# One head and two blocks at a time: another shape of the score matmuls in a fused attention and two-MLP kernel

## The chip, the cores and the metric

The kernel runs on one core of one Trainium2 chip. The metric is the device time of one execution in microseconds (us). Three runs of the kernel before gave 885.55, 885.6 and 886.19 us, median 885.6.

## The reference

The program is a chain of three parts. Attention has 4 batches, 8 heads, 576 positions and head dimension 64, with a mask by blocks of 64: a query sees every key of its own block and of the blocks before it. Its output, 2304 rows of 512, goes through a layer with three input matrices, the elementwise maximum of the three products and an output matrix, and then through a layer with g = h * cos(h).

```python
scores = scale * np.matmul(q, k.transpose(0, 1, 3, 2))
mask = block_i >= block_j                      # block = position // 64
scores = np.where(mask, scores, -1000000000.0)
scores = scores - np.max(scores, axis=-1, keepdims=True)
attn = np.exp(scores)
attn = attn / (np.sum(attn, axis=-1, keepdims=True) + 1e-09)
x = np.matmul(attn, v)                         # then reshaped to (2304, 512)
h = np.maximum(np.maximum(x @ w1, x @ w2), x @ w3)
x = h @ w_out                                  # 512 -> 768 -> 512
h = x @ w_in
out = (h * np.cos(h)) @ w_out2                 # 512 -> 2048 -> 512
```

All data is fp32. The two layers and most scores are computed with each fp32 operand split in a high and a low part of type fp32r: high times high, high times low and low times high, three matmuls that add up in one PSUM tile.

## The kernel before

**How attention is tiled.** An item is one batch, one pair of heads and one half of the queries; there are 32, numbered by batch, then half, then pair. In batch one (b = 0) the halves are blocks 0 to 4 and 5 to 8; in the other three batches they are blocks 0 to 3 and 4 to 8 (the table `HALF`, lines 549 to 562). This text calls them the early and the later queries.

For a block of 64 queries, `q` is laid out in 128 columns: 64 of the first head, with zeros in the rows of the second, and 64 of the second, with zeros in the rows of the first. One matmul of that 128x128 operand against the keys of both heads (head one in rows 0 to 63, head two in 64 to 127) gives the scores of both heads for one block, and runs only over the keys that the block sees, 64 (b + 1) columns. No mask is needed. `scores` (line 611) makes three matmuls for each block (`qh` with `kh`, `qh` with `kl`, `ql` with `kh`), or one in plain fp32 for the first ten items (`NATIVE`, tiles `qnat` and `knat`). The scores stand in the PSUM tiles SA (two banks) and SB (one bank), one buffer each. VectorE takes the maxima (`top`), ScalarE the exponentials (`prob`, one tile for each block, and `sums`), and the rows are then scaled.

`transposes` (line 655) turns `prob` by 128x128 TensorE transposes, four to a PSUM tile `tb`, copied into `pt`: 6 for an item with blocks 0 to 3 and 19 for one with blocks 4 to 8. `pv` (line 668) multiplies `pt` with v (`vr`) in plain fp32 into the PSUM tile X: the first head into rows 0 to 63, the second into rows 64 to 127, which the profile shows as matmuls of form 128*64 instead of 128*128. Such a group is called a visit to v here. From batch two on, the early queries of two pairs share one visit (`twin`, `pv(items[n - 2], it)`).

**What else runs.** The first layer's matmuls (tile `psm`, function `moe1_units`) are interleaved with attention, a chunk of tokens as soon as its attention is done. The second layer follows (`psm` and `po`). Weights come from memory and are split by VectorE and ScalarE (`convert`, tiles `raw`, `t`, `whi`, `wlo`). `load` (line 579) brings q, k and v of an item two items ahead; `q`, `k`, `kh`, `kl`, `qh` and `ql` have one buffer each. `prep` (line 599) makes the high and low parts.

**What sets the order.** All operations are recorded first, each with its engine or engines, a price and the operations it needs. A planner (class `Plan`) then schedules the list several times forward and backward (`PASSES`), keeps the shortest plan by its prices, and issues the instructions of each engine in that order, which is fixed from then on. A group marked `unit()` stays together. The price of a visit to v holds 350 ns beside its matmuls (`SWITCH`, line 686); that of a transpose is 109 ns. All instructions are issued from the helper in line 214, so that they are told apart in the profile by their tiles.

Of the kernel before, what the change touches and what calls it, by code (L numbers as in the profile page):

```python
# [8 lines left out]
F32 = mybir.dt.float32  # L9
# [10 lines left out]
P = 128  # L20
# [5 lines left out]
def f32(ap):  # L26
    return ap.bitcast(F32)
# [102 lines left out]
class Plan:  # L130
# [155 lines left out]


    ENGINES = ("PE", "DVE", "ACT", "POOL", "SP")
    PASSES = 8

    def after(self, d, o, stop):
        if d.engine == "PE" and o.engine == "PE":
# [13 lines left out]
    def forward(self, rank):  # L306
# [6 lines left out]
        end, chosen, bus, port = {}, {}, 0.0, 0.0  # L313

        def finish(o, start, stop):
            nonlocal left
            left -= 1
# [24 lines left out]
        left = len(self.ops)  # L342
        for o in self.ops:
            if not o.deps:
                release(o)
        while left:
            best = None
            for e in free:
                while waiting[e] and waiting[e][0][0] <= free[e]:
                    at, r, order, o = heapq.heappop(waiting[e])  # L350
                    heapq.heappush(ready[e], (r, order, at, o))
                if ready[e]:
                    t, pick = free[e], ready[e][0]
                    if pick[3].port and port > t:
                        others = [x for x in ready[e] if not x[3].port]
                        if others:
                            pick = min(others)
                        else:
                            t = port
                elif waiting[e]:  # L360
                    pick = waiting[e][0]
                    t = max(pick[0], port if pick[3].port else 0.0)
                else:
                    continue
                if best is None or t < best[0]:
                    best = (t, e, pick)
            assert best, "the plan has a cycle"
            t, e, pick = best
            o = pick[3]
            if ready[e]:  # L370
                ready[e].remove(pick)
                heapq.heapify(ready[e])
            else:
                heapq.heappop(waiting[e])
            free[e] = t + self.spent(o, t)
            load[e] -= o.cost
            stop = free[e] + o.late
            if o.port:
                port = free[e]
            if e == "SP":  # L380
                bus = max(bus, t + o.cost)
                bus += (o.late - 2000.0) * (1.22 if bus < self.SLOW else 1.0)
                stop = bus + 2000.0
            finish(o, t, stop)
# [73 lines left out]
                fn()  # L458


def fused_kernel(tc, qk, v2, w1, w2, w3, wout, w_in2, w_out2, out):
    B, HP, _, S = qk.shape
    S //= 3
    D = P // 2
# [79 lines left out]
    class Half:  # L544
        pass

    HALF = []
    for first, last, *tiles in (  # L550
# [5 lines left out]
        f = Half()  # L556
        f.first, f.blocks, f.tiles = first, list(range(first, last)), tiles
        f.n = 64 * (last - first)
        f.nk = 64 * last
        f.nj = (last + 1) // 2  # L560
        f.order = [(j, b) for j in range(f.nj) for b in f.blocks if 64 * (b + 1) > 128 * j]
        HALF.append(f)
    NATIVE = 10

    items = []
    for b in range(B):
        for half in range(2):
            for pair in range(HP):
                it = Item()
                it.b, it.half, it.pair, it.n, it.f = b, half, pair, len(items), HALF[half + 2 * (b > 0)]  # L570
# [4 lines left out]
    prob = [at.tile([P, (b // 2 + 1) * P], F32, f"prob{b}") for b in range(S // 64)]  # L575
    for b in range(0, S // 64, 2):
        R.gpsimd.memset(prob[b][:, 64 * (b + 1):], 0.0)

    def load(it):
# [8 lines left out]
        nlow = 2 * HALF[2 * (it.b > 0)].n  # L588
        q0 = nlow + S if it.half else 0
        R.sync.dma_start(it.q, src[:, q0:q0 + nq])  # L590
        R.sync.dma_start(it.k, src[:, nlow:nlow + f.nk])
        if it.n == 0:
            conv_next()
        it.j0 = f.nj if it.twin and it.pair % 2 else 0
        it.vr = items[it.n - 1].vr if it.j0 else at.tile([P, 5, 2, 64], F32, "vr", tag="vr", bufs=2)
        R.sync.dma_start(it.vr[:, it.j0:it.j0 + f.nj].rearrange("p j a d -> p j (a d)"),
                         v2[it.b, it.pair, :, 0:f.nj])

    def prep(it):
        f = it.f  # L600
        if it.native:
            R.scale(it.k, it.k, scale)
            return
# [4 lines left out]
        R.scale(it.qh, it.q, scale)  # L608
        R.vector.scalar_tensor_tensor(it.ql, it.q, scale, f32(it.qh), ALU.mult, ALU.subtract)

    def scores(it):

        f = it.f
        sm = sums[it.n % NROT]
        nb = len(f.blocks)
# [37 lines left out]
            R.scale_rows(p, p, sm[:, i:i + 1])  # L653

    def transposes(it):
        order = it.f.order
        it.c0 = len(order) if it.j0 else 0
        it.pt = items[it.n - 1].pt if it.j0 else at.tile([P, 19, P], F32, "pt", tag="pt")
        for c in range(0, len(order), 4):
            part = order[c:c + 4]  # L660
            n = P * len(part)
# [4 lines left out]
            R.copy(it.pt[:, it.c0 + c:it.c0 + c + len(part)].rearrange("p b n -> p (b n)"), t[:, :n])  # L666

    def pv(*its):
        f = its[0].f
# [4 lines left out]
        X = ps_x.tile([P, 512], F32, "X", tag="X")  # L674
        with R.unit():
            for x, it in enumerate(its):
                for j in range(f.nj):
                    c0, b0 = where[j][0]
                    q0 = 64 * (b0 - f.first)
                    for e in range(2):  # L680
                        a = 64 * e
                        p = it.pt[:, it.c0 + c0:it.c0 + c0 + len(where[j]), a:a + 64]
                        R.tensor.matmul(X[a:a + 64, x * n + q0:x * n + n], it.vr[:, it.j0 + j, e], p,
                                        start=x == 0 and j == 0, stop=x == len(its) - 1 and j == f.nj - 1,
                                        skip_group_check=True)
            R.unit_op.cost += R.SWITCH
        t0 = S * it.b + HALF[2 * (it.b > 0)].n * it.half
        for x, it in enumerate(its):
            xs = None
            for c, to, frm, m in pieces(t0, n):  # L690
                src = X[:, x * n + frm:x * n + frm + m]
                if c == 0:
                    h, l = xhi[0][it.pair][:, to:to + m], xlo[0][it.pair][:, to:to + m]
                    R.copy(h, src)
                    R.vector.tensor_tensor(l, src, f32(h), ALU.subtract)
                else:
                    xs = xs or at.tile([P, NLOW], F32, "xs", tag="xs", bufs=2)
                    R.copy(xs[:, frm:frm + m], src)
                    R.sync.dma_start(x_dram[c][it.pair][:, to:to + m], xs[:, frm:frm + m])

    def load_x(c, k):
        n = parts[c][1]
# [114 lines left out]
    for n in range(NI + 1):  # L817
        if n:
            transposes(items[n - 1])
        for step in range(3):  # L820
# [3 lines left out]
                    load(items[n + LA])  # L824
            if step == 2 and n:
                it = items[n - 1]
                if not it.twin:
                    pv(it)
                elif it.j0:
                    pv(items[n - 2], it)  # L830
                if it.n == HP - 1:
                    R.close(cv_start)
                    wk = R.open(cv_start, name="wk", bufs=1)
                done = S * it.b + (S if it.half else it.f.n) if it.pair == HP - 1 else 0
# [181 lines left out]
```

## Time and profile before

| | us |
|---|---|
| median of three runs | 885.6 |
| profiled execution, its own time | 885.22 |
| span of its trace, first to last instruction | 883.4 |
| TensorE (PE) busy | 868.1 |
| VectorE (DVE) busy | 540.9 |
| ScalarE (ACT) busy | 440.7 |
| GpSimd (POOL) busy | 1.2 |

The busy time of PE counts a matmul from its start to its modelled end, and ends overlap the next starts: a matmul of 512 columns is shown with some 390 ns, while the next starts 227 ns later. How long the engine is held by one instruction is therefore read from the start of one row of the timeline to the start of the next, not from the mean durations. In the timeline, equal neighbours are merged into one row with xN. A plain fp32 matmul is two instructions there, a transpose is one. After a group of transposes the next matmul is shown with an early start and a longer stay.

### The profile page before, as it was taken

To read this page: it belongs to the slowest core of one execution; us is meant where nothing else is said; L and a number is where in the kernel's file an instruction comes from. 1 tells how busy PE (TensorE), PEld (TensorE's weight loads), DVE (VectorE), ACT (ScalarE), POOL (GpSimd) and SP (SyncE) were. 2 spreads that over 40 slices of the span, in tenths; PEclk is the share of its full clock that TensorE was granted. 3 is DMA by queue.
4 is the path that set the end of the run, shared out by engine and by line. 5 is a ranking of instruction groups with operands and counts; after the bars stand their busy time and mean duration, and the time that the engine had idled before them with its cause. 6 is when DMAs were issued, how large, how long until landed. Compare 5 with 4: busy or idle time off the path is not lost.

```text
span 883.4 us, 12430 instructions
## 1 busy us (share of the span) xinstructions
PE 868.1 (98%) x4618; PEld 721.1 (82%) x4618; DVE 540.9 (61%) x1072; ACT 440.7 (50%) x969; POOL 1.2 (0%) x12
## 2 busy tenths in 40 slices
PE   7899999999999999999999999999999999999998
PEld 5568888888888888888899888888888888888897
DVE  6999986774566635628522897645564555555454
ACT  7997687853777627845321543332233223322333
POOL 0000000000000000000000000000000000000000
PEclk9999999999999999999999999999999999999999
DMA  7765545662256503355030931110001000100000
GB/s 259 233 203 174 151 151 175 217 228 77 75 155 220 207 1 106 129 171 167 23 122 17 354 130 48 48 48 1 0 24 49 1 0 1 48 1 0 25 24 24
DMA packets 42396, 90.33 MB, mean 102 GB/s; under 512 B 5728, under 2 KB 15456, under 8 KB 42336
## 3 DMA queue, kind: packets, MB, share of 16 engines
q1 hardware_dynamic: 42336, 89.54, 31.0%
q8 instruction: 36, 0.59, 0.3%
q14 instruction: 24, 0.20, 0.1%
HBM read 69.07 MB, written 20.45 MB: 101 GB/s over the span
## 4 chain that ended last, share of the span: by engine, by line
PE 93%; DVE 3%; ACT 2%; DMA 1%; issue 0%; POOLq 0%; POOL 0%; ACTq 0%
PE psm L214 56%; PE po L214 22%; PE X L214 4%; PE tb L214 4%; PE SA L214 4%; PE SB L214 3%; ACT prob L214 1%; DVE t L214 1%; DVE top L214 1%; DMA raw<-w 0%; ACT pt L214 0%; DVE prob L214 0%; DMA knat<-qk 0%; ACT t L214 0%; DVE whi L214 0%
## 5 line engine op out<-in xcount | busy, mean ns | idle before, releaser
L214 PE MATMUL psm<-yh,w_in 128*128 128x512 f32 (+1 forms) x640 | 194.2, 368 | 0.0
L214 PE MATMUL po<-w_out,gh 128*128 128x512 f32 x576 | 177.7, 390 | 0.0
L214 ACT ACTIVATE th<-th,halfpi 128x512 f32<-128x512 f32 (+1 forms) x80 | 54.5, 682 | 189.0 <-DVE th L214 189.0
L214 PE MATMUL psm<-xhi,whi 128*128 128x512 f32 (+1 forms) x360 | 135.4, 376 | 0.0
L214 PEld LDWEIGHTS psm<-yh,w_in 128*128 128x128 f32 x640 | 117.1, 188 | 20.8
L214 PE MATMUL psm<-xhi,wlo 128*128 128x512 f32 (+1 forms) x360 | 132.7, 369 | 0.0
L214 PE MATMUL psm<-xlo,whi 128*128 128x512 f32 (+1 forms) x360 | 132.6, 368 | 0.0
L214 PEld LDWEIGHTS po<-w_out,gh 128*128 128x128 f32 x576 | 107.1, 188 | 21.3
L214 PE MATMUL psm<-yl,w_in 128*128 128x512 f32 (+1 forms) x320 | 117.7, 368 | 0.0
L214 PE MATMUL po<-w_out,gl 128*128 128x512 f32 x288 | 112.0, 389 | 0.0
L214 DVE TENSOR_SCALAR th<-psm 128x512 int32<-128x512 f32 (+1 forms) x80 | 51.0, 637 | 76.4 <-PE psm L214 76.2
L214 DVE TENSOR_TENSOR th<-psm,th 128x512 f32<-128x512 f32 (+1 forms) x80 | 51.0, 637 | 53.7 <-ACT th L214 53.7
L214 DVE TENSOR_TENSOR hm<-psm,hm 128x512 f32<-128x512 f32 (+1 forms) x60 | 38.1, 634 | 66.7 <-PE psm L214 64.8
L214 PEld LDWEIGHTS psm<-xhi,wlo 128*128 128x128 f32 x360 | 67.9, 189 | 11.5
L214 PEld LDWEIGHTS psm<-xhi,whi 128*128 128x128 f32 x360 | 68.0, 189 | 10.3 <-issue 0.3
L214 PEld LDWEIGHTS psm<-xlo,whi 128*128 128x128 f32 x360 | 68.0, 189 | 9.8
L214 DVE TENSOR_TENSOR gl<-th,gh 128x512 fp32r<-128x512 f32 (+1 forms) x80 | 50.9, 636 | 38.3 <-ACT gh L214 38.3
L214 ACT CAST gh<-th 128x512 fp32r<-128x512 f32 (+1 forms) x76 | 44.0, 578 | 55.7 <-DVE th L214 55.7
L214 PEld LDWEIGHTS psm<-yl,w_in 128*128 128x128 f32 x320 | 60.3, 188 | 10.5
L214 ACT COPY pt<-tb 128x512 f32<-128x512 f32 (+1 forms) x96 | 52.9, 570 | 21.4 <-PE tb L214 20.9
L214 PEld LDWEIGHTS po<-w_out,gl 128*128 128x128 f32 x288 | 54.1, 188 | 11.4
L214 PE MATMUL tb<-ident,prob 128*128 128x128 f32 x400 | 57.6, 276 | 2.6 <-ACT pt L214 1.8
(96 smaller groups left out, 1305.0 us busy)
## 6 DMA issues: line engine op xcount, KB each, us to landing
raw<-w SPq DMA_DIRECT2D x18, 512.0 KB, 3.7
raw<-w_in SPq DMA_DIRECT2D x16, 512.0 KB, 4.0
raw<-w_out SPq DMA_DIRECT2D x16, 512.0 KB, 4.5
vr<-v SPq DMA_DIRECT2D x16, 320.0 KB, 3.4
kept_in<-both SPq DMA_DIRECT2D x10, 512.0 KB, 3.1
w_in<-kept_in SPq DMA_DIRECT2D x10, 512.0 KB, 9.9
out<-osb SPq DMA_DIRECT2D x18, 256.0 KB, 2.0
y<-hm SPq DMA_DIRECT2D x16, 256.0 KB, 2.8
```

The lines of the kernel that those rows point to most:

```text
L214: return lambda: getattr(real, method)(*[value(a) for a in args], **{k: value(a) for k, a in kw.items()})
```

## The change

From batch two on the halves are blocks 0 to 4 and 5 to 8, as in batch one, and the later queries (now four blocks) are computed in another way; their items are called stacked. q comes in 256 columns for each head (four blocks of 64), the same 64 rows twice. The scaled high part stands in `qh` rows 0 to 63 and the low part in rows 64 to 127; k of one head, twice too, is in `kh`. One matmul of `qh` with `kh` then gives high times high plus low times high. A second, `ql` with `kl`, has the high part of q and the low part of k in rows 0 to 63, and in rows 64 and 96 a mask: -2^100 in q's columns of the earlier block of two, 1 in the last 64 keys. A matmul takes two blocks of one head (128 columns of q) against all keys that the later block sees: blocks 5 and 6 against 448 keys in SB, blocks 7 and 8 against 576 keys in SA.

The two heads of an item follow each other: k of the second head has a load of its own and the same single-buffered tiles `k`, `kh` and `kl`. `kl` and `ql` stay in place over the four pairs of a batch, and their mask rows are set by GpSimd once for each batch. The transposes of a stacked item are 18, nine for each head: groups of four 128x128, and groups of five, of which two turn only the rows 64 to 127 of a tile, because the other rows are masked. Each item has its own visit to v. The planner makes 30 passes instead of 8.

```diff
-    PASSES = 8
+    PASSES = 30
...
+    PAIRS = ((0, P, 7 * 64, (6, 7)), (P, 2 * P, S, (8, 5)))
+    NEVER = -2.0 ** 100
...
-                it.twin = b > 0 and not half
                 it.native = it.n < NATIVE
+                it.stacked = b > 0 and half == 1
...
+            if it.stacked:
+                it.k = [it.k, at.tile([P, S], F32, "k", tag="k")]
...
+            for e in range(2):
+                R.sync.dma_start(it.k[e], k1[it.b - 1, it.pair, :, e * S:e * S + S])
...
+    def prep_k(it, e):
+        it.kh = at.tile([P, S], F32R, "kh", tag="kh")
+        R.copy(it.kh, it.k[e])
+        R.sub(it.kl[0:64], it.k[e][0:64], f32(it.kh[0:64]))
+
+    def prep_stacked(it):
...
+        it.qh = at.tile([P, 5 * P], F32R, "qh", tag="qh")[:, :4 * P]
+        R.scale(it.qh, it.q, scale)
+        R.copy(it.ql[0:64], f32(it.qh[0:64]))
+        R.vector.scalar_tensor_tensor(it.qh[64:P], it.q[64:P], scale, f32(it.qh[64:P]), ALU.mult, ALU.subtract)
+        prep_k(it, 0)
+
+    def scores_stacked(it):
+        sm = sums[it.n % NROT]
+        for e in range(2):
+            if e:
+                prep_k(it, 1)
...
+            for x, (q0, q1, nk, where) in enumerate(PAIRS):
...
+                for bank in range(c):
+                    with R.unit():
+                        for i, (q, k) in enumerate(((it.qh, it.kh), (it.ql, it.kl))):
+                            R.tensor.matmul(s[:, bank, 0:n], q[:, qs], k[:, bank * n:bank * n + n], start=i == 0,
+                                            stop=i == 1, skip_group_check=True)
...
+    def transposes_stacked(it):
+        it.pt = at.tile([P, 16 * P], F32, "pt", tag="pt")
+        for e in range(2):
+            a, b = (prob[where[e]] for *_, where in PAIRS)
+            for h in range(2):
+                tiles = [(a, 2 * h, 0), (b, 2 * h, 0)] + (
+                    [(a, 1, 0), (b, 1, 0)] if h == 0 else [(a, 3, 64), (b, 3, 0), (b, 4, 64)])
+                t = ps_x.tile([P, 512], F32, "tb", tag="T", bufs=2)
+                with R.unit():
+                    c0 = 0
+                    for p, j, r in tiles:
+                        R.tensor.transpose(t[:, c0:c0 + P - r], p[r:P, j * P:j * P + P], ident[r:P, r:P])
+                        c0 += P - r
+                c = 1024 * e + 512 * h
+                R.copy(it.pt[:, c:c + 512], t)
+
+    def pv_stacked(it):
+        X = ps_x.tile([P, 512], F32, "X", tag="X")
+        with R.unit():
+            for j, (c0, m) in enumerate(((0, 256), (256, 256), (512, 256), (768, 192), (960, 64))):
+                for e in range(2):
+                    p = it.pt[:, 1024 * e + c0:1024 * e + c0 + m]
+                    R.tensor.matmul(X[64 * e:64 * e + 64, 256 - m:256], it.vr[:, j, e], p, start=j == 0, stop=j == 4,
+                                    skip_group_check=True)
+            R.unit_op.cost += R.SWITCH
+        return X
...
-                if not it.twin:
-                    pv(it)
-                elif it.j0:
-                    pv(items[n - 2], it)
+                pv(it)
```

The three places below are all on TensorE. First the scores of an item of later queries in batch two. Before, SA holds blocks 8 (288 columns in each of two banks) and 6 (224), three matmuls each:

```order
L214 MATMUL SA<-kh,qh 128x288
L214 MATMUL SA<-kl,qh 128x288
L214 MATMUL SA<-kh,ql 128x288
L214 MATMUL SA<-kh,qh 128x224
L214 MATMUL SA<-kl,qh 128x224
L214 MATMUL SA<-kh,ql 128x224
L214 MATMUL SA<-kh,qh 128x288
L214 MATMUL SA<-kl,qh 128x288
L214 MATMUL SA<-kh,ql 128x288
L214 MATMUL SA<-kh,qh 128x224
L214 MATMUL SA<-kl,qh 128x224
L214 MATMUL SA<-kh,ql 128x224
```

Now the scores of the second head of a stacked item: two matmuls of 448 in SB, and twice two of 288 in SA.

```order
L214 MATMUL SB<-kh,qh 128x448
L214 MATMUL SB<-kl,ql 128x448
L214 MATMUL SA<-kh,qh 128x288
L214 MATMUL SA<-kl,ql 128x288
L214 MATMUL SA<-kh,qh 128x288
L214 MATMUL SA<-kl,ql 128x288
```

The three products of a block have become two of a pair of blocks, and what followed for blocks 7, 5 and 4 in further tiles is in these six as well.

Second, the transposes of such an item. Before, three groups of four and more stand between the scores, all of the whole 128 rows:

```order
L214 MATMUL tb<-ident,prob_430 128x128
L214 MATMUL tb<-ident,prob_102 128x128
L214 MATMUL tb<-ident,prob_98 128x128
L214 MATMUL tb<-ident,prob_463 128x128
```

Now the two groups of one head in batch two, with the matmuls of the first layer around them (a row of form 128x64 turns 64 rows):

```order
L214 MATMUL psm<-xhi_503,wlo_1_1128 128x512
L214 MATMUL tb<-ident,prob_100 128x128
L214 MATMUL tb<-ident,prob_102 128x128
L214 MATMUL tb<-ident,prob_100 128x128
L214 MATMUL tb<-ident,prob_102 128x128
L214 MATMUL tb<-ident,prob_100 128x128
L214 MATMUL tb<-ident,prob_102 128x128
L214 MATMUL tb<-ident,prob_100 128x64
L214 MATMUL tb<-ident,prob_102 128x128
L214 MATMUL tb<-ident,prob_102 128x64
L214 MATMUL psm<-xhi_255,whi_2_1144 128x512
```

The second group has five transposes instead of four, and the third and the fifth of it are of 64 rows.

Third, the visit to v of early queries in batch two, before with two items in it:

```order
L214 MATMUL psm<-xhi_2217,wlo_0_1069 128x512
L214 MATMUL X<-pt,vr 64x256 x2
L214 MATMUL X<-pt,vr 64x128 x2
L214 MATMUL X<-pt,vr 64x256 x2
L214 MATMUL X<-pt,vr 64x128 x2
L214 MATMUL tb<-ident,prob_98 128x128
```

And now with one item, of five blocks:

```order
L214 MATMUL SA<-kl,ql 128x288
L214 MATMUL X<-pt,vr 64x320 x2
L214 MATMUL X<-pt,vr 64x192 x2
L214 MATMUL X<-pt,vr 64x64 x2
L214 MATMUL psm<-xhi_503,whi_2_1144 128x512
```

The visit holds three pairs of matmuls in place of four, and there are two such visits for one before.

## Rows read from the trace of the kernel before

**Rows 1.** The page, part 1: busy us, share of the span, instructions by engine.

```profile
PE 868.1 (98%) x4618; PEld 721.1 (82%) x4618; DVE 540.9 (61%) x1072; ACT 440.7 (50%) x969; POOL 1.2 (0%) x12
```

**Rows 2.** Windows, core 0: each engine's busy us, granted TensorE clock, DMA.

```profile
0.00:75.00 75.00, 63.32 (x391) 46.79 (x392) 66.89 (x178) 67.23 (x181) 1.17 (x12) 1.00 0.71 226
75.00:395.00 320.00, 320.00 (x1867) 263.62 (x1866) 205.11 (x438) 212.83 (x517) 0.00 (x0) 1.00 0.47 150
395.00:875.00 480.00, 480.00 (x2344) 407.06 (x2343) 267.45 (x455) 158.51 (x268) 0.00 (x0) 1.00 0.15 52
875.00:883.00 8.00, 4.78 (x22) 3.60 (x20) 1.41 (x4) 2.09 (x4) 0.00 (x0) 0.98 0.18 66
```

**Rows 3.** Timeline, PE, one visit to v: start us, duration us, instruction.

```profile
239.23 0.39 PE L214 MATMUL psm<-xhi,whi 128*128 128x512 f32 x1
239.46 0.39 PE L214 MATMUL psm<-xlo,whi 128*128 128x512 f32 x1
239.68 0.39 PE L214 MATMUL psm<-xhi,wlo 128*128 128x512 f32 x1
240.00 2.27 PE L214 MATMUL X<-pt,vr 128*64 128x320 f32 x20
242.21 0.40 PE L214 MATMUL SA<-kh,qh 128*128 128x288 f32 x1
242.44 0.30 PE L214 MATMUL SA<-kl,qh 128*128 128x288 f32 x1
242.58 0.29 PE L214 MATMUL SA<-kh,ql 128*128 128x288 f32 x1
```

**Rows 4.** Timeline, PE, scores of a later-queries item and the transposes behind.

```profile
257.19 0.29 PE L214 MATMUL SA<-kh,qh 128*128 128x288 f32 x1
257.32 0.29 PE L214 MATMUL SA<-kl,qh 128*128 128x288 f32 x1
...
257.58 0.27 PE L214 MATMUL SA<-kh,qh 128*128 128x224 f32 x1
257.69 0.28 PE L214 MATMUL SA<-kl,qh 128*128 128x224 f32 x1
...
257.91 1.04 PE L214 MATMUL tb<-ident,prob 128*128 128x128 f32 x8
258.70 0.38 PE L214 MATMUL SA<-kh,qh 128*128 128x288 f32 x1
258.92 0.29 PE L214 MATMUL SA<-kl,qh 128*128 128x288 f32 x1
```

**Rows 5.** Timeline, PE, narrower scores of a later-queries item.

```profile
249.30 0.34 PE L214 MATMUL SB<-kh,qh 128*128 128x384 f32 x1
249.48 0.34 PE L214 MATMUL SB<-kl,qh 128*128 128x384 f32 x1
...
249.83 0.32 PE L214 MATMUL SB<-kh,qh 128*128 128x320 f32 x1
...
250.29 0.39 PE L214 MATMUL psm<-hh,vhi 128*128 128x512 f32 x1
```

**Rows 6.** Timeline, PE, plain fp32 scores of batch one.

```profile
16.18 1.08 PE L214 MATMUL SB<-knat,qnat 128*128 128x320 f32 x4
17.09 1.04 PE L214 MATMUL tb<-ident,prob 128*128 128x128 f32 x8
```

**Rows 7.** Groups by form: busy us, mean ns of one, idle before.

```profile
L214 DVE TENSOR_TENSOR kl<-k,kh 128x576 fp32r<-128x576 f32 x12 | 9.0, 754 | 1.1 <-ACT kh L214 1.1
L214 ACT CAST kh<-k 128x576 fp32r<-128x576 f32 x12 | 8.0, 670 | 4.5 <-PE SB L214 4.4 <-PE SA L214 0.2
L214 DVE SCALAR_TENSOR_TENSOR ql<-q,qh 128x512 fp32r<-128x512 f32 x10 | 6.8, 681 | 0.0
L214 POOL MEMSET prob<- 128x64 f32 x5 | 0.6, 153 | 0.0
```

**Rows 8.** Tile k: time from issue to landing of its 22 loads.

```profile
DMA to landing us min/median/max: 2.1/2.8/6.2
```

More of the change, by code (lines that the diff above doesn't have):

```diff
@@ L315, in finish @@
         def finish(o, start, stop):
-            nonlocal left
-            left -= 1
             end[o] = (start, stop)
@@ L340, in release @@
             heapq.heappush(waiting[o.engine], (at, rank[o], o.order, o))
-        left = len(self.ops)
         for o in self.ops:
@@ L345, in forward @@
                 release(o)
-        while left:
+        while len(end) < len(self.ops):
             best = None
@@ L549, in fused_kernel @@
     HALF = []
-    for first, last, *tiles in (
[5 rows of a table removed]
-        f = Half()
[L557 to L560, printed above, removed]
+    for u in range(2):
+        f = Half()
+        f.n = NHIGH if u else NLOW
+        f.first = 5 if u else 0
+        f.blocks = list(range(5, 9)) if u else list(range(0, 5))
+        f.nk = S if u else NLOW
+        f.nj = 5 if u else 3
+        f.both = 0 if u else 128
         f.order = [(j, b) for j in range(f.nj) for b in f.blocks if 64 * (b + 1) > 128 * j]
+        f.tiles = ((2, ((8, 0, 288, 2), (6, 288, 224, 2))), (1, ((7, 0, 512, 1),)), (1, ((5, 0, 384, 1),))) if u else (
+            (1, ((4, 0, 320, 1), (2, 320, 192, 1))), (0, ((3, 0, 256, 1), (1, 256, 128, 1), (0, 384, 64, 1))))
         HALF.append(f)
+    PAIRS = ((0, P, 7 * 64, (6, 7)), (P, 2 * P, S, (8, 5)))
+    NEVER = -2.0 ** 100
     NATIVE = 10
@@ L569, in fused_kernel @@
                 it = Item()
-                it.b, it.half, it.pair, it.n, it.f = b, half, pair, len(items), HALF[half + 2 * (b > 0)]
-                it.twin = b > 0 and not half
+                it.b, it.half, it.pair, it.n, it.f = b, half, pair, len(items), HALF[half]
                 it.native = it.n < NATIVE
+                it.stacked = b > 0 and half == 1
                 items.append(it)
-    prob = [at.tile([P, (b // 2 + 1) * P], F32, f"prob{b}") for b in range(S // 64)]
+    prob = [at.tile([P, (9 if b == 5 else b) // 2 * P + P], F32, f"prob{b}") for b in range(S // 64)]
     for b in range(0, S // 64, 2):
         R.gpsimd.memset(prob[b][:, 64 * (b + 1):], 0.0)
+    R.gpsimd.memset(prob[5][:, S:], 0.0)
     def load(it):
@@ L587, in load @@
             it.k = at.tile([P, S], F32, "k", tag="k")[:, :f.nk]
-        nlow = 2 * HALF[2 * (it.b > 0)].n
-        q0 = nlow + S if it.half else 0
+            if it.stacked:
+                it.k = [it.k, at.tile([P, S], F32, "k", tag="k")]
+        q0 = 2 * NLOW + S if it.half else 0
         R.sync.dma_start(it.q, src[:, q0:q0 + nq])
-        R.sync.dma_start(it.k, src[:, nlow:nlow + f.nk])
+        if it.stacked:
+            for e in range(2):
+                R.sync.dma_start(it.k[e], k1[it.b - 1, it.pair, :, e * S:e * S + S])
+        else:
+            R.sync.dma_start(it.k, src[:, 2 * NLOW:2 * NLOW + f.nk])
         if it.n == 0:
             conv_next()
[L594 to L597, printed above, removed]
+        it.vr = at.tile([P, 5, 2, 64], F32, "vr", tag="vr", bufs=2)
+        R.sync.dma_start(it.vr[:, 0:f.nj].rearrange("p j a d -> p j (a d)"), v2[it.b, it.pair, :, 0:f.nj])
     def prep(it):
         f = it.f
+        if it.stacked:
+            return prep_stacked(it)
         if it.native:
@@ L609, in prep @@
         R.vector.scalar_tensor_tensor(it.ql, it.q, scale, f32(it.qh), ALU.mult, ALU.subtract)
+    def prep_k(it, e):
[3 more added lines that the diff above has]
+    def prep_stacked(it):
+        if it.pair:
+            it.kl, it.ql = items[it.n - 1].kl, items[it.n - 1].ql
+        else:
+            it.kl = at.tile([P, S], F32R, "kl", tag="kl")
+            it.ql = at.tile([P, 5 * P], F32R, "ql", tag="ql")[:, :4 * P]
+            for t in (it.kl, it.ql):
+                R.gpsimd.memset(f32(t[64:P]), 0.0)
+            for x, (q0, q1, nk, _) in enumerate(PAIRS):
+                row = slice(64 + 32 * x, 65 + 32 * x)
+                R.gpsimd.memset(f32(it.kl[row, nk - 64:nk]), 1.0)
+                for e in range(2):
+                    R.gpsimd.memset(f32(it.ql[row, 2 * P * e + q0:2 * P * e + q0 + 64]), NEVER)
+            if it.b == 1:
+                R.gpsimd.memset(prob[7][:, 7 * 64:], 0.0)
+        it.qh = at.tile([P, 5 * P], F32R, "qh", tag="qh")[:, :4 * P]
[3 more added lines that the diff above has]
+        prep_k(it, 0)
@@ new lines, in transposes_stacked @@
+    def transposes_stacked(it):
+        it.pt = at.tile([P, 16 * P], F32, "pt", tag="pt")
+        for e in range(2):
+            a, b = (prob[where[e]] for *_, where in PAIRS)
[10 more added lines that the diff above has]
+                R.copy(it.pt[:, c:c + 512], t)
@@ new lines, in pv_stacked @@
+    def pv_stacked(it):
+        X = ps_x.tile([P, 512], F32, "X", tag="X")
+        with R.unit():
+            for j, (c0, m) in enumerate(((0, 256), (256, 256), (512, 256), (768, 192), (960, 64))):
+                for e in range(2):
+                    p = it.pt[:, 1024 * e + c0:1024 * e + c0 + m]
[3 more added lines that the diff above has]
+        return X
@@ L611, in scores @@
     def scores(it):
+        if it.stacked:
+            return scores_stacked(it)
         f = it.f
@@ L655, in transposes @@
     def transposes(it):
+        if it.stacked:
+            return transposes_stacked(it)
         order = it.f.order
-        it.c0 = len(order) if it.j0 else 0
-        it.pt = items[it.n - 1].pt if it.j0 else at.tile([P, 19, P], F32, "pt", tag="pt")
+        it.pt = at.tile([P, 16, P], F32, "pt", tag="pt")
         for c in range(0, len(order), 4):
@@ L665, in transposes, with pv @@
                     R.tensor.transpose(t[:, x * P:x * P + P], prob[b][:, j * P:j * P + P], ident)
-            R.copy(it.pt[:, it.c0 + c:it.c0 + c + len(part)].rearrange("p b n -> p (b n)"), t[:, :n])
-    def pv(*its):
-        f = its[0].f
+            R.copy(it.pt[:, c:c + len(part)].rearrange("p b n -> p (b n)"), t[:, :n])
+    def pv(it):
+        f = it.f
         n = f.n
@@ L673, in pv @@
             where.setdefault(j, []).append((c, b))
-        X = ps_x.tile([P, 512], F32, "X", tag="X")
-        with R.unit():
-            for x, it in enumerate(its):
+        if it.stacked:
+            X = pv_stacked(it)
+        else:
+            X = ps_x.tile([P, 512], F32, "X", tag="X")
+            with R.unit():
                 for j in range(f.nj):
@@ L681, in pv @@
                         a = 64 * e
-                        p = it.pt[:, it.c0 + c0:it.c0 + c0 + len(where[j]), a:a + 64]
-                        R.tensor.matmul(X[a:a + 64, x * n + q0:x * n + n], it.vr[:, it.j0 + j, e], p,
-                                        start=x == 0 and j == 0, stop=x == len(its) - 1 and j == f.nj - 1,
+                        p = it.pt[:, c0:c0 + len(where[j]), a:a + 64]
+                        R.tensor.matmul(X[a:a + 64, q0:n], it.vr[:, j, e], p, start=j == 0, stop=j == f.nj - 1,
                                         skip_group_check=True)
[L686 to L699, printed above, removed]
+                R.unit_op.cost += R.SWITCH
+        t0 = S * it.b + NLOW * it.half
+        xs = None
+        for c, to, frm, m in pieces(t0, n):
+            src = X[:, 0 + frm:0 + frm + m]
+            if c == 0:
+                h, l = xhi[0][it.pair][:, to:to + m], xlo[0][it.pair][:, to:to + m]
+                R.copy(h, src)
+                R.vector.tensor_tensor(l, src, f32(h), ALU.subtract)
+            else:
+                xs = xs or at.tile([P, NLOW], F32, "xs", tag="xs", bufs=2)
+                R.copy(xs[:, frm:frm + m], src)
+                R.sync.dma_start(x_dram[c][it.pair][:, to:to + m], xs[:, frm:frm + m])
     def load_x(c, k):
@@ L833, in fused_kernel @@
                     wk = R.open(cv_start, name="wk", bufs=1)
-                done = S * it.b + (S if it.half else it.f.n) if it.pair == HP - 1 else 0
+                done = S * it.b + (S if it.half else NLOW) if it.pair == HP - 1 else 0
                 while begun[0] < len(parts) and sum(parts[begun[0]]) <= done:
@@ L995 @@
     qd = qd.reshape(B, H // 2, P, 2 * S)
+    last = heads.reshape(B, H // 2, 2, D, S)[1:, ..., NLOW:].transpose(0, 1, 3, 2, 4).reshape(B - 1, H // 2, D, 2 * NHIGH)
+    qd[1:, :, :, 2 * NLOW:] = np.concatenate([last, last], axis=2)
+    k1 = kT[1:].reshape(B - 1, H // 2, 2, D, S).transpose(0, 1, 3, 2, 4).reshape(B - 1, H // 2, D, 2 * S)
     kT = kT.reshape(B, H // 2, P, S)
-    low = [2 * NLOW] + [2 * NHIGH] * (B - 1)
     arrays = {
-        "qk": np.stack([np.concatenate([qd[b, ..., :n], kT[b], qd[b, ..., n:]], axis=2) for b, n in enumerate(low)]),
+        "qk": np.concatenate([qd[..., :2 * NLOW], kT, qd[..., 2 * NLOW:]], axis=3),
+        "k1": np.concatenate([k1, k1], axis=2),
         "v2": np.ascontiguousarray(v2.reshape(B, H // 2, P, (S + D) // P, 2 * D)),
```

19 lines of the change are left out of this document (18 added, 1 removed), and 5 rows, old and new, of the table HALF.

## Prediction

> **What bounds the kernel now.** I read the page's engine shares first, then the busy time by stretches, then TensorE's timeline inside attention, and last the groups by form. The page shows PE busy in 98% of the span [rows 1]. By stretches the reader sees where the rest is [rows 2]: 11.7 us of the first 75 (75.00 less 63.32), nothing from 75 to 875 us, 3.2 us in the last eight. The granted clock is 1.00 from the start to 875 us, the upper level (2.4 GHz) throughout. The change begins with batch two, whose stacked items lie between about 100 us and the end of attention near 395 us. There PE is busy in 320.00 of 320 us, VectorE in 205 and ScalarE in 213. So PE sets the time in this stretch, and each us that an instruction holds PE, longer or shorter, moves the end by one us, as long as the others keep up. Busy time alone hides short gaps, so I count PE's time from start to start in the timeline.
>
> **Score matmuls.** The products of the first layer in front of a visit follow each other every 227 ns at 512 columns (239.23 to 239.68 for two) [rows 3]. Three of 288 columns take 0.39 us and three of 224 take 0.33 [rows 4]; three of 384 take 0.53 and three of 320 take 0.46 [rows 5]. An item of later queries before: block 7 (512) 0.68, block 5 (384) 0.53, block 4 (320) 0.46, block 8 (six of 288) 0.78, block 6 (six of 224) 0.66, together 3.11 us. A stacked item: four of 448 and eight of 288. No row has 448; between 384 (0.177) and 512 (0.227) it is about 0.20. That is 0.80 + 1.04 = 1.84 us, 1.27 less, and with 12 items -15.2 us. Block 4 moves to the early queries: three of 320 more in ten items (+0.46 each, +4.6), and one plain fp32 product of 320 columns more in the two native items of batch two. Two plain products of 512 columns together take 0.91 us [rows 6], so 320 are 0.57, +1.1 for both. Sum of the scores: -9.5 us.
>
> **Transposes.** Eight take 0.88 us (257.91 to 258.92, less the 0.13 of the 288 between), 0.11 each [rows 4]. A pair of items had 6 + 19 and has 9 + 18, two more in each of 12, 24 in all: +2.6 us at 0.109. Half-height ones could be cheaper; if the 48 of them took half the time, the term would be nothing. Their weight operand is still 128 columns wide, so I take 2.6 and keep 0 as the other end.
>
> **Visits to v.** The columns stay the same: 384 + 1216 for both halves before, 576 + 1024 now. Not so the visits: three batches had 2 + 4 each and have 8, six more. The price of one is in the timeline [rows 3]: its first matmul starts 0.32 us behind the last of 512 instead of 0.227 (+0.09); from there to the next score it is 2.21 us, where 1216 columns (the two heads run beside each other) are 2.03 at 2.4 GHz with the four passes of plain fp32 that [rows 6] show, 0.91 us for 512 columns against 0.85 of pure columns (+0.18); and the second score starts 0.23 behind the first instead of 0.13 (+0.10). That is 0.37 us beyond its columns, +2.2 us for six.
>
> So far the sum is -9.5 + 2.6 + 2.2 = -4.7 us.
>
> **Half-height transposes.** This is the term that decides. The trace has no matmul of 64 rows, but it has one change of form, from 128*128 to 128*64 and back, in every visit, and there PE pays 0.37 us [rows 3]. About 0.07 of it belongs to the ten column steps inside (a matmul of 512 holds PE 14 ns longer than its 213 of columns, five times in a row); the remaining 0.30 is the change to the other form and back. The group of five in each head's transposes goes full, full, half, full, half, and then full again in what follows: two such returns. There are 24 of these groups (12 items, two heads). If a half of the rows costs what a half of the columns costs, that is 2 x 0.30 x 24 = 14.4 us, at most 2 x 0.37 x 24 = 17.8. If it costs nothing, 0. I take 14.4, since the visit is the only row in which the array changes form, and keep 0 and 17.8 as ends.
>
> The Trainium skill, page TensorEngine Tiling (Array Packing), section Key Properties, says that changing the tiling mode, and not just the tile, drains TensorE, and its list of modes has 64x128 beside 128x64. The visits of this trace agree for 128x64 (0.37 us) and no row shows 64x128; by that rule the sum is the one with 14.4, without it the one at -4.7.
>
> **What is hidden.** The second head's k adds work elsewhere. A `kl` of 576 columns takes 0.75 us on VectorE, a `kh` 0.67 on ScalarE, a low part of q of 512 columns 0.68 [rows 7]. For each pair VectorE gets one more subtraction of 576 and a few shifts in width, about 1.2 us, ScalarE about 0.7; in 12 pairs 15 and 9 us. VectorE has 115 us idle between 75 and 395, ScalarE 107 [rows 2]; cost zero while PE has first-layer matmuls between the heads, and it has them or transposes in all three orders shown. If that cover were gone, PE would wait for the chain of the next paragraph. The memsets of the mask rows (about eight for each batch) run on an idle POOL, 0.15 us for 64 columns [rows 7]; 576 columns might take 1.4, behind some 6 us of PE's work: zero. The first 75 us hold the same batch one, but two native items with a block more and another plan of 30 passes; with PE idle there for 11.7 us I put 0, and 2.5 us to either side.
>
> Sum: -4.7 + 14.4 = +9.7 us on the profiled execution's 885.22, 894.9; the median of three is 0.4 above that execution, so 895.
>
> **Rivals.** (a) The form of half the rows costs nothing; then only -4.7 is left: 885.6 - 4.7 = 880.9, or 878.3 if those transposes are also half as long. For it: the weights of a 128*128 matmul load under the one before (512 columns follow at 227 ns), and if that goes on from 128 rows to 64, nothing drains. Against it: at the entry of a visit nothing was loaded in time, 0.09 us later than usual. This is the case on the other side, and it decides where a return costs under 0.06 us (2.9 us in 48). (b) The return costs about a third, 0.10 us: 48 x 0.10 = 4.8, which eats the gain: 885.7, no change. (c) The single k buffer: the second head's k can only be loaded when the first head's has been read, so the two heads' scores stand at least a landing (2.8 us, up to 6.2 [rows 8]) + 0.67 + 0.75 apart, 4.2 to 7.6 us. If PE's own work between them is about 5 us, a late landing costs up to 2.6 in each of 12 items, 31 at worst; at half of them 1.5 late it is 9 us: without the mode price 880.9 + 9 = 890. For it: PE's order is fixed. Against it: the same buffers are refilled for each item before, and PE never waited after 75 us [rows 2].
>
> **How the numbers follow.** The forecast, both returns paid: 0.64, its own range 889 to 899 (0.20 us for a return gives +4.9, 0.37 gives +13.1, and some of the 2.5 us of the start on the low side). Rival (a) 0.22, (b) 0.08, (c) without the mode price 0.06. About 0.2% of 885.6, 1.8 us, is what a measurement of this kernel can tell from no change. Faster by more than that is (a), 0.22. Within it are (b) and the edge of the forecast where a return is cheap and the first 75 us get shorter, 0.09. Slower is the rest of the forecast and (c), 0.69. Cases of both signs have weight, so the range reaches from most of (a) to the dear end of the forecast: 880 to 899.
>
> **What would show it.** In the trace after, a transposes group with form 64*128 in it: from its first start to the start of the second matmul behind it, some 0.6 us more than five times 0.11 if the returns are paid. Right too: two matmuls of 288 at 0.13 each, 448 at 0.20, visits at 0.37 beyond their columns. Wrong would be a PE that waits between 75 and 395 us for `kh` or `kl` (rival c), an idle time of the first 75 us off 11.7 by more than 2.5, or half-height transposes that follow at 0.11 like the others (rival a).

## The result, and the profile after

The changed kernel took 894.0 us in the median of 6 runs (892.65 to 897.07) against 885.58 for the kernel before (885.24 to 886.19): a ratio of 1.0101, 95% interval 1.0081 to 1.0121. It is about 1% slower. The profiled execution took 892.99 us with a span of 891.2; it stands 7.8 us behind the profiled execution before (885.22), where +9.7 was forecast. Part of the spread between single runs goes with the granted clock (892.65 and 892.99 us at a mean of 0.999, 896.74 and 897.07 at 0.994); the last section shows where it fell in other runs.

The page, part 1, of the kernel after, answers to [rows 1]:

```profile
PE 876.3 (98%) x4616; PEld 720.7 (81%) x4616; DVE 556.1 (62%) x1099; ACT 450.7 (51%) x974; POOL 6.5 (1%) x38
```

The windows of the kernel after (each engine's busy us and instructions, granted clock, DMA share, GB/s), answer to [rows 2]:

```profile
0.00:75.00 75.00, 63.72 (x390) 47.51 (x391) 65.85 (x177) 65.49 (x174) 1.42 (x14) 1.00 0.69 223
75.00:395.00 320.00, 320.00 (x1782) 258.39 (x1780) 209.71 (x439) 205.37 (x490) 5.08 (x24) 1.00 0.47 150
395.00:875.00 480.00, 480.00 (x2376) 404.07 (x2376) 273.89 (x467) 174.97 (x302) 0.00 (x0) 1.00 0.18 62
875.00:891.00 16.00, 12.58 (x73) 10.76 (x71) 6.63 (x17) 4.84 (x10) 0.00 (x0) 0.98 0.09 33
```

The reader is to see three things. First, TensorE is still without a gap from 75 to 875 us, at the upper level of the clock. Second, its idle time in the first 75 us is 11.28 us where it was 11.68, so nothing was lost at the start. Third, VectorE and ScalarE together are no busier between 75 and 395 than they were (210 and 205 us against 205 and 213). This points to TensorE's own work, in a stretch in which it hardly waits, as what moved the end; the experiments test it.

The scores of one head of a stacked item, timeline of the kernel after (start us, duration us, instruction):

```profile
110.54 0.36 PE L214 MATMUL SB<-kh,qh 128*128 128x448 f32 x1
110.74 0.37 PE L214 MATMUL SB<-kl,ql 128*128 128x448 f32 x1
110.94 0.29 PE L214 MATMUL SA<-kh,qh 128*128 128x288 f32 x1
111.08 0.29 PE L214 MATMUL SA<-kl,ql 128*128 128x288 f32 x1
111.21 0.29 PE L214 MATMUL SA<-kh,qh 128*128 128x288 f32 x1
111.34 0.29 PE L214 MATMUL SA<-kl,ql 128*128 128x288 f32 x1
111.47 0.40 PE L214 MATMUL psm<-xhi,whi 128*128 128x512 f32 x1
```

448 columns hold TensorE for 0.20 us and 288 for 0.13, as the sum had it. One head takes 0.93 us (110.54 to 111.47), so both take 1.86, where the five blocks took 3.11 [rows 4, 5].

A visit to v of a stacked item:

```profile
140.27 0.29 PE L214 MATMUL SA<-kl,ql 128*128 128x288 f32 x1
140.50 1.96 PE L214 MATMUL X<-pt,vr 128*64 128x256 f32 x20
142.38 0.50 PE L214 MATMUL psm<-hh,vhi 128*128 128x512 f32 x1
142.72 0.39 PE L214 MATMUL psm<-hl,vhi 128*128 128x512 f32 x1
```

From the point at which the next matmul would normally start (140.27 + 0.13) to the visit it takes 0.10 us. The visit itself takes 1.88 us for 1024 columns, which are 1.71 at four passes, so 0.17 more. The second matmul behind it starts 0.34 us after the first instead of 0.23, so 0.11 more. That is 0.38 us beyond the columns, against 0.37 in [rows 3].

Now the transposes. The group of five of one head, in the same timeline:

```profile
147.75 0.30 PE L214 MATMUL SA<-kl,ql 128*128 128x288 f32 x1
147.88 1.04 PE L214 MATMUL tb<-ident,prob 128*128 128x128 f32 x5
148.86 0.40 PE L214 MATMUL SA<-kh,qh 128*128 128x288 f32 x1
149.10 0.29 PE L214 MATMUL SA<-kl,ql 128*128 128x288 f32 x1
149.23 0.39 PE L214 MATMUL psm<-hh,vhi 128*128 128x512 f32 x1
```

Five transposes were 0.11 us each in [rows 4]. Here the first of five and the next matmul stand 0.98 us apart, and the next but one is late by another 0.11 (0.24 instead of 0.13): 1.09 us in place of 0.55, so 0.54 us more. The timeline merges the five under the form of the first. Narrower windows of the same timeline show the third, the fourth and the fifth by themselves:

```profile
148.20 0.27 PE L214 MATMUL tb<-ident,prob 64*128 64x64 f32 x1
148.40 0.33 PE L214 MATMUL tb<-ident,prob 128*128 128x128 f32 x1
148.66 0.27 PE L214 MATMUL tb<-ident,prob 64*128 64x64 f32 x1
```

Two full transposes take 0.22 us from 147.88, to 148.10; the first of 64 rows starts 0.10 us later than that. Then the starts are 0.20, 0.26 and 0.20 us apart instead of 0.11. So TensorE is late at each change of form, on the way to 64 rows as well as on the way back. The answer for the tile tb names the form of 142 of its 424 transposes:

```profile
L214 PE MATMUL tb<-ident,prob x424: 270/272/332, 11.0 to 441.5; 128*128 128x128 f32 x118, 64*128 64x64 f32 x24
```

And the list of waits between 75 and 870 us has a row that was hardly there before (0.3 us, twice): the weight load of a transpose that waits for nothing but its engine (us, times, longest):

```profile
PEld X L214 <- issue: 5.4, 17, 0.4
PEld tb L214 <- issue: 4.0, 24, 0.2
```

There are 24 such waits for 24 groups; the other row is the same wait at the visits to v. The row does not count all changes of form: the trace of e2_side_by_side below, with half as many, has the same one (4.0 us, 24 times). All 24 groups of this trace, read like the one above, give 0.53 to 0.60 us each and 13.0 us together.

### The profile page after: what moved, and what is told of

Read it like the earlier page. It is cut to its first block, busy times and chain, and to the rows that moved or that the text cites. A ratio compares the mean times of both kernels' runs of the same rounds, so it can differ in the third digit from the quotient of the medians.

```text
span 891.2 us, 12524 instructions
## 1 busy us (share of the span) xinstructions
PE 876.3 (98%) x4616; PEld 720.7 (81%) x4616; DVE 556.1 (62%) x1099; ACT 450.7 (51%) x974; POOL 6.5 (1%) x38
## 4 chain that ended last, share of the span: by engine, by line
PE 95%; ACT 2%; DMA 1%; DVE 1%; issue 0%; SPq 0%; ACTq 0%; DVEq 0%
PE psm L214 56%; PE po L214 22%; PE tb L214 6%; PE X L214 5%; PE SA L214 3%; PE SB L214 3%; DMA raw<-w 1%; ACT prob L214 1%; ACT pt L214 0%; SPq L214 0%; DVE t L214 0%; DVE top L214 0%; ACT add L214 0%; DVE prob L214 0%; ACT t L214 0%
## 5 line engine op out<-in xcount | busy, mean ns | idle before, releaser
L214 PE MATMUL psm<-xhi,whi 128*128 128x512 f32 (+1 forms) x360 | 137.2, 381 | 0.0
L214 PEld LDWEIGHTS psm<-xhi,wlo 128*128 128x128 f32 x360 | 67.9, 189 | 11.8
L214 PE MATMUL tb<-ident,prob 128*128 128x128 f32 (+1 forms) x424 | 68.4, 278 | 3.4 <-ACT pt L214 2.9
L214 ACT COPY pt<-tb 128x512 f32<-128x512 f32 (+1 forms) x101 | 55.9, 568 | 23.6 <-PE tb L214 23.1
L214 PEld LDWEIGHTS tb<-ident,prob 128*128 128x128 f32 (+1 forms) x424 | 51.1, 140 | 20.3 <-issue 5.2
```

The lines of the kernel that those rows point to most:

```text
L214: return lambda: getattr(real, method)(*[value(a) for a in args], **{k: value(a) for k, a in kw.items()})
```

## The experiments

Seven kernels were run, each against the kernel before on the same chip: the first four on one chip, the last three on another. The change itself was timed in the runs told above. The last column is the fastest run whose mean granted clock was 0.999 or more.

| kernel | median us (runs) | ratio to before, 95% interval | fastest at full clock |
|---|---|---|---|
| before, beside the first four | 885.68 (20) | | 884.99 |
| the change | 894.0 (6) | 1.0101 (1.0081 to 1.0121) | 892.65 |
| e1_full_height | 882.22 (6) | 0.996 (0.9945 to 0.9976) | none (881.14 at 0.998) |
| e2_side_by_side | 887.3 (12) | 1.0014 (1.0001 to 1.0026) | 885.62 |
| e4_eight_passes | 895.31 (6) | 1.0105 (1.0088 to 1.0122) | 893.77 |
| e6_before_own_visits | 890.96 (9) | 1.005 (1.0035 to 1.0066) | 887.71 |
| before, beside the last three | 885.91 (18) | | 884.51 |
| e5_before_30 | 884.49 (12) | 0.9989 (0.998 to 0.9999) | 883.72 |
| e7_full_height_8 | 883.05 (6) | 0.9967 (0.9956 to 0.9978) | 881.56 |
| e8_filled_start | 881.79 (5) | 0.9954 (0.9942 to 0.9966) | 880.78 |

**Transposes of full height (e1_full_height).** The 48 transposes of 64 rows become transposes of 128 rows. Their first 64 columns are not wanted, so each is made before its left neighbour, which overwrites them. Nothing else in the recorded operations changes.

```diff
-                    c0 = 0
+                    c0, placed = 0, []
                     for p, j, r in tiles:
-                        R.tensor.transpose(t[:, c0:c0 + P - r], p[r:P, j * P:j * P + P], ident[r:P, r:P])
+                        placed.append((-r, c0 - r, p, j))
                         c0 += P - r
+                    for _, c0, p, j in sorted(placed, key=lambda x: x[:2]):
+                        R.tensor.transpose(t[:, c0:c0 + P], p[:, j * P:j * P + P], ident)
```

> The change, with its 48 transposes of 64 rows made as transposes of all 128 rows: each is done before its left neighbour, which then overwrites the 64 columns it does not need. The number and the order of all instructions on all engines stay the same but for the place inside each group of five. Theory 1 (each return from the 64-row form to the full form holds TensorE, about 0.27 us for each of the 48 as read from the trace of the change): 13 us less than the change, so about 880 to 881.5, some 5 us faster than the kernel before; a group of five takes 5 x 0.11 = 0.55 us. Theory 2 (the loss is in the new plan and in the chain of the second head's k, and the longer transposes only stand where TensorE would wait anyway): 892 to 895, as the change, with waits of TensorE for SA, SB or kh in place of the gaps.

Measured: 882.22 us, 11.8 less than the change and 0.4% less than the kernel before. The timeline of the same group of five:

```profile
147.41 0.30 PE L214 MATMUL SA<-kl,ql 128*128 128x288 f32 x1
147.55 0.71 PE L214 MATMUL tb<-ident,prob 128*128 128x128 f32 x5
148.01 0.38 PE L214 MATMUL SA<-kh,qh 128*128 128x288 f32 x1
148.23 0.30 PE L214 MATMUL SA<-kl,ql 128*128 128x288 f32 x1
148.37 0.39 PE L214 MATMUL psm<-hh,vhi 128*128 128x512 f32 x1
```

The group takes 0.46 us and the second matmul behind it is 0.09 late (0.22 instead of 0.13): 0.55 us, five times 0.11. The waits between 75 and 870 us no longer have the row of tb; the visits to v still have theirs:

```profile
PEld X L214 <- issue: 5.8, 18, 0.4
```

Theory 1 holds and theory 2 falls: the operations, the loads of k and the plan's 30 passes are those of the change, only the form and the place of the transposes inside each group differ, and the loss is gone. The median is 0.7 us above the range given; no run of it had the full clock.

**The two side by side (e2_side_by_side).** The same five transposes, with the two of 64 rows at the end.

```diff
-                    c0 = 0
+                    c0, placed = 0, []
                     for p, j, r in tiles:
-                        R.tensor.transpose(t[:, c0:c0 + P - r], p[r:P, j * P:j * P + P], ident[r:P, r:P])
+                        placed.append((r, c0, p, j))
                         c0 += P - r
+                    for r, c0, p, j in sorted(placed, key=lambda x: x[:2]):
+                        R.tensor.transpose(t[:, c0:c0 + P - r], p[r:P, j * P:j * P + P], ident[r:P, r:P])
```

> The change, with the two transposes of 64 rows of each group at its end, one behind the other, so that the group goes from the full form to the other one and back once instead of twice; nothing else moves. Theory 1 (the price belongs to the change of form, 0.27 us there and back): half of the 13 us goes, 886.5 to 888. Theory 1b (the price belongs to each transpose of 64 rows, whatever stands beside it): no change, 892 to 895. Theory 2 (plan and waits): no change, 892 to 895.

Measured: 887.3 us, in the range of theory 1. The group in its timeline:

```profile
146.69 0.29 PE L214 MATMUL SA<-kl,ql 128*128 128x288 f32 x1
146.82 0.75 PE L214 MATMUL tb<-ident,prob 128*128 128x128 f32 x5
147.50 0.40 PE L214 MATMUL SA<-kh,qh 128*128 128x288 f32 x1
147.74 0.29 PE L214 MATMUL SA<-kl,ql 128*128 128x288 f32 x1
147.87 0.40 PE L214 MATMUL psm<-hh,vhi 128*128 128x512 f32 x1
```

The group takes 0.68 us and the second matmul behind it is 0.11 late: 0.79 us, 0.24 beyond five times 0.11. So two changes of form and back cost 0.54, one costs 0.24, none costs nothing. The two of 64 rows, each in a narrow window of this timeline:

```profile
147.24 0.27 PE L214 MATMUL tb<-ident,prob 64*128 64x64 f32 x1
147.35 0.22 PE L214 MATMUL tb<-ident,prob 64*128 64x64 f32 x1
```

They start 0.11 us apart, like full ones: what is paid is the change of form, and a transpose of 64 rows as such costs neither more nor less than another. Theory 1b falls. The end moved as the groups say: 24 times 0.30 us are 7.2, and the fastest runs at full clock of the change and of this kernel stand 7.0 us apart (892.65 and 885.62).

**Eight passes instead of thirty (e4_eight_passes, e5_before_30, e7_full_height_8).** One line, `PASSES`, is altered: in the change, in the kernel before and in e1_full_height.

> The change with the planner's 8 passes instead of 30, all operations the same. Theory 1 (TensorE's own work sets the time from 75 us on, and the order matters only in the first 75 us): 892 to 896.5, within 2.5 us of the change, the transposes' gaps as before. Theory 2 (the plan is what costs): 886 to 889.

> The kernel before with the planner's 30 passes instead of 8, the other half of the question of the plan. Theory 1 (from 75 us on TensorE's work sets the time, the plan matters in the first 75 us alone): 883 to 888. Theory 2 (30 passes find a worse order on the chip, and that is the change's loss): 891 to 894.

> The change with transposes of full height (as in e1_full_height) and the planner's 8 passes. Theory 1: 881 to 884, the same as with 30 passes within the 2.5 us of the start. Theory 2 (the plan matters beyond the start): more than 3 us away from e1_full_height.

Measured: 895.31, 884.49 and 883.05 us. The change with 8 passes is not apart from the change with 30 (the intervals overlap), nor e7 from e1. The kernel before gains about 1 us by 30 passes, 0.9989 with an interval that just excludes 1. So the plan is worth about one us, and in the direction opposite to the loss. It is not a matter of the first 75 us alone, as theory 1 of e4 had it: there the 8 passes leave TensorE idle for 9.93 us, less than the 11.28 of the 30, but behind them TensorE waits once for `pt`, in e4 and in e7, as the list of waits from 75 to 870 us shows:

```profile
PE X L214 <- ACT pt L214: 1.9, 1, 1.9
```

The two kernels with 8 passes give the price of the form once more: at full clock e7 took 881.56 us and e4 893.77, 12.2 apart, on two chips on which the kernel before differs by 0.5.

**Visits of their own in the kernel before (e6_before_own_visits).**

```diff
-                it.twin = b > 0 and not half
+                it.twin = False
```

> The kernel before, with a visit to v of its own for each item of early queries, one part of the change alone: six visits more, the same columns. Theory 1 (each visit holds TensorE for 0.37 us beyond its columns and nothing hides it): 2 to 2.3 us more, 887.6 to 888. Rival (the visit's extra is hidden or planned away): 885.3 to 886.2, no change.

Measured: 890.96 us in the median, 5.3 more and outside the range of theory 1. The two runs at full clock took 887.71 and 887.86, which is 2.3 to 2.5 us more than the runs of the kernel before at full clock (885.2 to 885.6 for most): the 2.2 us of six visits. The other seven had a granted clock of 0.996 or 0.994, and the trace of one of them shows where it fell (last section). The price of a visit is supported by these two runs and by the visit's own rows; the median alone would not show it.

**A filled start (e8_filled_start).** e1_full_height with 32 small matmuls more that nothing reads, for TensorE's idle time in batch one.

```diff
             transposes(items[n - 1])
+            if n <= 8:
+                for _ in range(4):
+                    idle = ps_m.tile([P, 512], F32, "psm", tag="M", bufs=2)
+                    with R.unit():
+                        R.tensor.matmul(idle[:, 0:P], ident, items[n - 1].q[:, 0:P], start=True, stop=True)
```

> As e1_full_height, with 32 groups of one small matmul more (ident times the first 128 columns of q, into a psm tile that nothing reads) that the planner may put into TensorE's idle time of batch one. Runs of e1_full_height whose granted clock is below 0.998 are up to 3.4 us longer than those at 0.998, and in its profile the clock is at its lower level from 16.0 to 19.4 us, behind a stretch in which TensorE was idle for 4.9 of 16 us. Theory 1 (TensorE's idle time in the first 41 us is what lowers the clock): the granted clock is 0.999 or above in most runs and the time 879.5 to 882, the spread of the runs under 2 us. Rival (the clock falls whatever TensorE does): the same spread of 881 to 885 as e1_full_height; third case, the small matmuls hold up the scores behind them: 882 to 886 at a clock of 0.999.

Measured: 881.79 us, the lowest median of the table, 0.46% less than the kernel before. Granted clocks were 0.998 to 1.0 in five runs, against 0.993 to 0.998 in six of e1_full_height, and the spread was 2.7 us against 3.4. But e1 ran on the other chip; e7_full_height_8, on the same chip and without these matmuls, had 0.996 to 1.0 and a spread of 2.8 us. Theory 1's condition (under 2 us) was missed and the intervals of e1 and e8 overlap. So whether the idle time lowers the clock is not settled.

## Why the prediction was right

The forecast was 895.0 us, the range 880 to 899, slower with 0.69; measured 894.0. The range alone says little, since it holds rival (a)'s 880.9 as well; what the runs support is the mechanism and the sign. Point by point:

- **TensorE sets the time from 75 to 875 us: right.** 320.00 of 320 us busy before and after, and what e1, e2 and e6 took off or added to its own work came out at the end, to about one us. One reading was off without harm: in the changed kernel the last transposes stand at 441.5 us and not before 395, and TensorE has no gap there either.
- **Scores -9.5 us: right in its parts.** 0.20 for 448 columns and 0.13 for 288 are in the trace; a stacked item takes 1.86 us where 1.84 was worked out. The whole term was not measured by itself.
- **Visits to v +2.2 us: right.** 0.38 us in the trace after, and 2.3 to 2.5 us for six in the two runs of e6 at full clock.
- **Transposes +2.6 us: right.** Full-height groups hold TensorE for 0.11 us for each transpose in e1. That 64-row ones might be half as long can be dropped: where two of them stand together, in e2, they start 0.11 us apart.
- **The change of form +14.4 us: right mechanism, a tenth too dear.** It was priced by the visits at 0.60 for a group and measured 0.54 (24 groups, 13.0 us; between runs at full clock 12.2, e4 against e7). The visits' matmuls have half of the columns, the transposes half of the rows; the change and the return cost nearly the same. How near is in part luck: the 0.07 us taken off for column steps was a choice. By [rows 6], 0.06 us for 512 columns, it would have been 0.14 for the visit's 1216, and the price 0.23 instead of 0.30; the measured 0.24 to 0.27 lies between. This is the one term that decided the sign. The Trainium skill, page TensorEngine Tiling (Array Packing), section Key Properties, says that a change of tiling mode drains TensorE. The trace after agrees, with 24 weight loads that wait for their engine alone and 0.54 us for two changes and returns.
- **Sum: +9.7 forecast, +7.8 between the profiled executions.** Of the 1.9 us between them, 13.0 instead of 14.4 explains 1.4, and the start, at 0.4 us less idle time, most of the rest.
- **Rival (a), no price for the form: wrong**, though its number (880.9) is what e1_full_height, which takes the changes of form out, comes to (882.22, and 881.14 in its fastest run). The rest of the sum, -4.7 us, is thereby measured too, to about one us: e1's profiled execution took 881.65, 3.6 less than that of the kernel before (885.22), and it lost at most 1.7 us to a stretch of 3.4 us at half clock.
- **Rival (b), a third of the price: wrong**; one change and return costs 0.24 to 0.27 us, not 0.10.
- **Rival (c), the chain of the second head's k: wrong here.** Its parts were sized right, a landing of 3.0 us in the middle and 6.8 at most, and a `kl` of 64 rows that takes as long as one of 128 [rows 7, 8]:

```profile
DMA to landing us min/median/max: 2.2/3.0/6.8
```

```profile
L214 DVE TENSOR_TENSOR kl<-k,kh 64x576 fp32r<-64x576 f32 x24 | 17.8, 744 | 1.1 <-ACT kh L214 1.0
```

  but TensorE hardly waited for it. Between 75 and 870 us the list of waits has one for `kl` at the scores, of 0.3 us:

```profile
PEld SB L214 <- DVE kl L214: 0.3, 1, 0.3
```

  In the timeline of the first stacked item the matmuls of the first layer stand between the heads, from 111.47 us on. The kernel was not run with a second k buffer.
- **Memsets: hidden. Plan: worth about one us (e4, e5).** The memsets of `kl` took 2.6 us of GpSimd in all, and they waited for TensorE; between 75 and 870 us TensorE has no wait for GpSimd:

```profile
L214 POOL MEMSET kl<- 1x64 f32 (+1 forms) x9 | 2.6, 289 | 267.8 <-PE SA L214 267.8
```

## What to carry to other kernels

Where one engine is busy without a gap, count what each instruction holds it, from start to start, and price a new form by the nearest change of form that the trace has: here a visit to v, off by a tenth. In this kernel a transpose of half the rows was no saving in the middle of full ones: the change of form and the return cost 0.24 to 0.27 us each time, more than two whole transposes. If the unwanted half can be overwritten, do the full one (e1); if not, put the half ones side by side (e2).

## What the runs showed of the hardware

The granted clock fell to the lower level (1.2 GHz) in some runs; in the traces that show it, it did so in the first 41 us, where TensorE waits for the other engines. Windows of e6_before_own_visits in its profiled execution, 892.46 us long:

```profile
0.00:13.70 13.70, 10.39 (x43) 8.23 (x43) 5.54 (x21) 8.34 (x24) 1.17 (x12) 1.00 0.82 278
13.70:20.50 6.80, 5.75 (x23) 4.30 (x24) 5.08 (x16) 4.70 (x15) 0.00 (x0) 0.50 0.54 183
20.50:37.60 17.10, 12.87 (x77) 8.90 (x76) 16.64 (x43) 16.20 (x50) 0.00 (x0) 1.00 0.66 218
37.60:41.00 3.40, 3.40 (x9) 1.46 (x9) 3.11 (x9) 2.68 (x5) 0.00 (x0) 0.50 0.35 135
41.00:75.00 34.00, 31.61 (x212) 22.96 (x210) 32.44 (x80) 29.97 (x73) 0.00 (x0) 1.00 0.54 184
```

The clock stands at 0.50 from 13.7 to 20.5 us, behind 13.7 us with TensorE busy for 10.39, and again from 37.6 to 41.0, behind 17.1 us with 12.87. In the first of these stretches VectorE and ScalarE are busy for 5.08 and 4.70 us of 6.8. The kernel before, in its profiled execution, kept its clock over the same time, and they were busy for 6.80 and 6.63:

```profile
0.00:13.70 13.70, 9.60 (x43) 7.65 (x43) 6.06 (x22) 8.98 (x25) 1.17 (x12) 1.00 0.81 277
13.70:20.50 6.80, 4.81 (x33) 3.70 (x34) 6.80 (x22) 6.63 (x23) 0.00 (x0) 1.00 0.80 266
```

In e1_full_height there is one such stretch, and in e8_filled_start none:

```profile
0.00:16.00 16.00, 11.07 (x55) 8.49 (x55) 8.02 (x27) 10.74 (x33) 1.27 (x13) 1.00 0.82 273
16.00:19.40 3.40, 3.39 (x10) 2.82 (x11) 2.32 (x8) 3.30 (x8) 0.00 (x0) 0.50 0.65 228
19.40:41.00 21.60, 17.42 (x105) 11.78 (x104) 21.20 (x57) 19.21 (x53) 0.00 (x0) 1.00 0.72 230
```

```profile
0.00:16.00 16.00, 13.21 (x77) 11.15 (x78) 8.14 (x27) 10.92 (x33) 1.27 (x13) 1.00 0.81 274
16.00:19.40 3.40, 3.40 (x29) 3.29 (x28) 3.40 (x12) 3.24 (x9) 0.00 (x0) 1.00 0.90 275
19.40:41.00 21.60, 19.27 (x130) 14.81 (x129) 21.60 (x55) 20.41 (x58) 0.00 (x0) 1.00 0.71 230
```

The price can be read from the runs: e6 took 887.7 to 887.9 us at 1.0, 890.7 to 891.0 at 0.996 and 892.1 to 892.5 at 0.994. The kernel before, beside it, has the same in a part of its runs (884.99 to 885.6 at 0.999 or more for most, 887.8 to 888.1 at 0.996). A difference of some 2 us between two kernels is therefore to be read at equal clock. Equal clock does not make runs equal: e4_eight_passes took 893.77 and 895.4 us, both at 1.0. What makes the clock fall was not settled. In the first 13.7 us TensorE was less busy in the kernel before, which kept its clock (9.60 us), than in e6, which lost it (10.39); in the first 16 us the kernel before (11.55) was nearly as idle as e1_full_height (11.07).
